# The sums of a float64 weight split move from GpSimd to TensorE and VectorE, and the state's decay to VectorE

## The chip, the cores and the metric

The kernel runs on one core of a Trainium2 chip. A core has TensorE (matrix products into PSUM, the accumulation memory), VectorE, ScalarE and GpSimd (arithmetic on SBUF, the on-chip memory of 128 partitions; VectorE and ScalarE read and write PSUM too), SyncE, which here only issues DMAs, and 16 DMA engines. The metric is the device time of one execution in microseconds, the median of three runs. In the profile TensorE's matmuls are called PE, its weight loads PEld, VectorE DVE, ScalarE ACT and GpSimd POOL.

## The reference

Three layers follow each other. All inputs are float32 but the dense layer's two weight matrices, which come as float64 values.

```python
# 1: attention with a decaying state, B=4, H=8, S=768, D=48
for t in range(S):
    kt, vt, rt, wt = k[:, :, t], v[:, :, t], r[:, :, t], w[:, :, t]
    cur = einsum('bhd,bhe->bhde', u[None] * kt, vt)
    y[:, :, t] = einsum('bhd,bhde->bhe', rt, state + cur)
    state = wt[:, :, :, None] * state + einsum('bhd,bhe->bhde', kt, vt)
x = y.transpose(0, 2, 1, 3).reshape(3072, 384)
# 2: dense layer, w_in 384x2048, w_out 2048x384
h = x @ w_in
x = (h * (1 / (1 + exp(-1.702 * h)))) @ w_out
# 3: eight experts (384 -> 1024 -> 384), 384 tokens each
logits = x @ w_gate       # all (token, expert) pairs, greatest first:
                          # a token goes to the first expert that has room
out[mask_e] = maximum(x[mask_e] @ w1[e], 0) @ w2[e]
```

## The kernel before

**Attention.** The 768 steps are cut into six chunks of 128; a chunk of one batch entry is a unit, 24 in all, each for all eight heads. Within a unit the products of the decays are formed by scans on VectorE (Q at L765, Fw at L769), k and r are scaled by them (L785, L788), and the state S of a batch entry (48 x 48 for each head) is carried from chunk to chunk: it is multiplied by the chunk's whole decay (L793, two instructions for the two halves of the heads) and the chunk's own part is added (L884). The three first units form the product r*k from what they have (L781), the others from a second copy of it in a tile nat_m (L812, L813, with u); its sums over a head (L815) are written on the diagonal of the score matrix by two `affine_select` masks on GpSimd (L822). A unit's result y goes into the dense layer as two fp32r tiles, hi (xh, L974, a rounding copy on ScalarE) and lo (xl, L977, the difference).

**Dense layer.** The 3072 tokens are eight blocks of 384, three units each. The hidden dimension is 16 slices of 128. A slot is one slice of one block: g1 (L1001, nine matmuls: three parts of the contraction by hi x hi, hi x lo, lo x hi), then the activation (L1047), its hi copy gh (L1050) and its difference gl on VectorE (L1053), and two slots later g2 (L1029, three parts of three matmuls, into acc). The slots come in this order: block 0 slices 0 to 7 (slots 0 to 7), block 1 (8 to 23), block 0 slices 8 to 15 (24 to 31), then blocks 2 to 7 (32 to 127). Slots 128 to 191 are the experts'.

**The float64 weights.** They come as 16 chunks of 128 x 768 (m = 0 to 15, w_in and w_out by turns, each good for two slices), and `split64` turns each into a hi and a lo tile in fp32r. The upper 32-bit words are rescaled (ScalarE L674, VectorE L678) and given their sign (L681); that is a, the value cut to its upper word. L687 and L688 form b, the part in the lower word. Then a + b (L692), hi = the rounding of it (ScalarE L696) and lo = (a + b) - hi (L699). At most two raw chunks are in flight; a is held in a ring of three tiles cvc, b in one of two cvb.

**The router's weights.** After the last chunk, `gate_weights` loads w_gate spread over the partitions, and `wog_steps` forms w_out times w_gate for each of the 16 slices: a sum hi + lo on GpSimd (L1137) and eight multiply-and-accumulate instructions on VectorE (L1141), 128 in all, then wogp (L1147, L1148). Block 7's matmuls begin only behind that.

**What sets the order.** The order of every engine's instructions is written at build time by a class `Issue`. It keeps a clock `t` and a time until which each engine is booked (`busy`: V, A, P for VectorE, ScalarE, GpSimd). The attention units, the chunks, the activations and the wog steps are chains of their own (Python generators), stepped by rank as the matmuls of the slots are laid down. `room(e, slack)` holds a chain until engine e is booked no further ahead than the slack. `either(lag, p, v)` gives an operation to GpSimd (cost p) or VectorE (cost v), whichever is done first by the booking, and by it L692, L699, L781, L785, L812 with L813 and L977 were placed. `until(cond)` holds the next slot's matmuls and puts a filler (`spin`, L638, a small bf16 matmul into an unused part of a bank) on TensorE for each 0.1 us of modelled waiting. On the chip only the order counts; the waits are by semaphores.

## Time and profile before

| | us |
|---|---|
| median of 3 runs | 937.81 |
| the runs | 935.88, 937.81, 937.83 |
| the profiled execution | 941.33 |
| its span, first to last instruction | 939.6 |
| TensorE busy (matmuls) | 882.1 (94%) |
| VectorE | 682.2 (73%) |
| ScalarE | 350.9 (37%) |
| GpSimd | 314.0 (33%) |
| mean granted TensorE clock | 0.947 |

The times are of one and the same kernel; the profiled execution has a time of its own, and sums over rows of its trace are to be set beside that. A share over the whole span says little here, since the stages have different limits; the stretches by slots are 41.6 to 97.8 us (slots 0 to 7), 97.8 to 128.0 (8 to 15), 128.0 to 195.1 (16 to 28), 195.1 to 519.8 (29 to 111), and what follows, which begins with the end of the router's weights.

### The profile page before, as it was taken

What the parts mean: (1) busy time and instruction counts of PE and PEld (TensorE: products, weight loads), DVE (VectorE), ACT (ScalarE), POOL (GpSimd) and SP (SyncE); (2) the same over time, 40 slices, a digit from 0 to 9 for tenths busy, and PEclk for the clock granted to TensorE, in tenths of its full rate; (3) what the DMA queues carried; (4) which work ended last, traced back from release to release, by engine and by line L of the source; (5) the groups of instructions that cost most, each with busy time, mean ns of one, the idle gap of its engine ahead of it and who ended that gap; (6) DMA issues with size and microseconds to landing.
All of it is one profiled execution on the core that took longest, in us unless ns stands there. A gap on an engine that the chain in (4) does not pass through costs nothing.

```text
span 939.6 us, 18095 instructions
## 1 busy us (share of the span) xinstructions
PE 882.1 (94%) x6867; PEld 834.0 (89%) x6867; DVE 682.2 (73%) x1791; ACT 350.9 (37%) x632; POOL 314.0 (33%) x319
## 2 busy tenths in 40 slices
PE   6977997999999999999999979989999989999995
PEld 5766996899999999999999979979889889899995
DVE  8699699799979789799797783666676776653210
ACT  1433553332333333333323034024554643657521
POOL 4477346512232324233223101021333423346311
PEclk8779999899999999999999999978898998899998
DMA  8526432423313222133210000058787977969900
GB/s 262 160 85 190 143 110 95 143 85 96 98 51 96 73 75 82 50 97 97 63 54 5 2 25 1 18 151 187 190 241 154 275 207 155 259 186 268 245 26 26
DMA packets 48504, 113.37 MB, mean 121 GB/s; under 512 B 7616, under 2 KB 13600, under 8 KB 48416
## 3 DMA queue, kind: packets, MB, share of 16 engines
q1 hardware_dynamic: 31680, 70.51, 23.8%
q0 software_dynamic: 12288, 34.61, 17.5%
q10 hardware_dynamic: 4448, 7.08, 2.2%
q8 instruction: 54, 0.88, 0.4%
q14 instruction: 34, 0.28, 0.1%
HBM read 75.95 MB, written 10.03 MB: 91 GB/s over the span
## 4 chain that ended last, share of the span: by engine, by line
PE 62%; DVE 20%; issue 9%; DMA 3%; POOL 2%; ACT 2%; ACTq 0%; DVEq 0%; POOLq 0%
PE g L1001 24%; PE acc L1029 22%; PE s L393 5%; DVE cvb L1078 3%; DVE cvb L1141 3%; PE s L920 2%; PE s L913 2%; DVE Q L765 2%; DVE gl L1053 2%; PE s L836 2%; DVE cvc L681 2%; PE acc L638 1%; DVE cvc L678 1%; PE s L453 1%; DMA hold<-in_w 1%
## 5 line engine op out<-in xcount | busy, mean ns | idle before, releaser
L1029 PE MATMUL acc<-wk,gh 128*128 128x384 f32 x1080 | 282.0, 341 | 0.3 <-ACT cva L1406 0.3
L1029 PEld LDWEIGHTS acc<-wk,gh 128*128 128x128 f32 x1080 | 196.5, 191 | 1.5 <-ACT cva L1406 0.6
L1029 PE MATMUL acc<-wk,gl 128*128 128x384 f32 x540 | 183.1, 339 | 0.0
L1001 PE MATMUL g<-xhb,wk 128*128 128x384 f32 x576 | 171.1, 350 | 11.0 <-DVE gl L1053 5.2
L1001 PE MATMUL g<-xha,wk 128*128 128x384 f32 x576 | 171.8, 350 | 6.9 <-DVE gl L1053 3.7
L1047 ACT ACTIVATE g<-g 128x384 f32<-128x384 f32 x128 | 60.8, 475 | 217.4 <-PE g L1001 195.4
L1001 PEld LDWEIGHTS g<-xhb,wk 128*128 128x128 f32 x576 | 108.8, 195 | 13.4 <-DVE gl L1053 5.6
L1001 PEld LDWEIGHTS g<-xha,wk 128*128 128x128 f32 x576 | 108.3, 193 | 10.7 <-DVE gl L1053 5.3
L1029 PEld LDWEIGHTS acc<-wk,gl 128*128 128x128 f32 x540 | 103.0, 191 | 0.0
L1001 PE MATMUL g<-xlb,wk 128*128 128x384 f32 x288 | 100.3, 348 | 0.0
L1001 PE MATMUL g<-xla,wk 128*128 128x384 f32 x288 | 99.4, 345 | 0.0
L1078 DVE SCALAR_TENSOR_TENSOR cvb<-cva,raw 128x384 f32<-128x384 f32 x168 | 95.6, 569 | 4.6 <-ACT cva L1117 1.5
L1053 DVE TENSOR_TENSOR gl<-g,gh 128x384 fp32r<-128x384 f32 x116 | 64.0, 551 | 39.3 <-ACT gh L1050 38.9
L1330 POOL DMA_DIRECT2D wk<-hold x64 | 57.6, 1045 | 85.3 <-ACT wk L1324 76.6
L1060 ACT ACTIVATE gh<-g 128x384 fp32r<-128x384 f32 x64 | 31.3, 489 | 129.0 <-PE g L1001 113.9
L1141 DVE SCALAR_TENSOR_TENSOR cvb<-cvb,raw 128x384 f32<-128x384 f32 x128 | 71.4, 557 | 10.8 <-POOL cvb L1137 5.1
L1063 DVE SCALAR_TENSOR_TENSOR gl<-g,gh 128x384 fp32r<-128x384 f32 x64 | 35.2, 552 | 60.7 <-ACT gh L1060 56.0
L793 POOL TENSOR_TENSOR S<-S,Q 48x192 f32<-48x192 f32 x40 | 49.4, 1235 | 88.6 <-DVE Q L765 87.1
L638 PE MATMUL acc<-ident 128*128 128x128 bf16 x842 | 60.1, 227 | 4.2 <-DVE ident L618 4.2
L638 PEld LDWEIGHTS <-ident 128*128 128x128 bf16 x842 | 51.4, 102 | 10.1 <-issue 5.1
L1050 ACT ACTIVATE gh<-g 128x384 fp32r<-128x384 f32 x116 | 56.9, 490 | 8.5 <-DVE cva L1112 3.2
L393 PEld LDWEIGHTS <-cvc 128*128 128x128 bf16 x840 | 53.3, 158 | 5.9 <-issue 2.6
(222 smaller groups left out, 1432.4 us busy)
## 6 DMA issues: line engine op xcount, KB each, us to landing
hold<-in_w SPq DMA_DIRECT2D x64, 384.0 KB
wk<-hold POOLq DMA_DIRECT2D x64, 384.0 KB
nat_m<-in_rk SPq DMA_DIRECT2D x20, 384.0 KB
raw<-in_w_in SPq DMA_DIRECT2D x8, 768.0 KB
raw<-in_w_out SPq DMA_DIRECT2D x8, 768.0 KB
nat_v<-in_v SPq DMA_DIRECT2D x22, 256.0 KB
nat_w<-in_w SPq DMA_DIRECT2D x22, 226.2 KB
nat_k<-in_k SPq DMA_DIRECT2D x22, 224.0 KB
```

What stands on the lines that cost most here:

```text
L393: nc.tensor.matmul(ps[:, :E], G[j], oh[:, j], start=(j == 0), stop=(j == NJ - 1))
L638: T.matmul(warm[0][:, Dm:], i16, i16, start=warm[1], stop=False, skip_group_check=True)
L793: P.tensor_tensor(h_, h_, Q[64 * s:64 * s + D, 1:HP * PW:PW, None].to_broadcast([D, HP, D]), op=OP.mult)
L1001: T.matmul(p, self.l1(kt, f, a), (self.xh, self.xl)[b_][:, kt], start=(kt == 0 and n == 0), stop=(kt == KT - 1 and n == 2))
L1029: T.matmul(self.acc[tt], gs[a][:, tt * C:(tt + 1) * C], self.r2(f, b_), start=(f in self.cuts and n == 0), stop=(end and n == 2))
L1047: A.activation(p, p, AF.Gelu_apprx_sigmoid)
L1050: A.activation(gh, p, AF.Copy)
L1053: V.tensor_tensor(gl, p, gh.bitcast(F32), op=OP.subtract)
L1063: V.scalar_tensor_tensor(gl, p, 0.0, gh.bitcast(F32), op0=OP.max, op1=OP.subtract)
L1078: V.scalar_tensor_tensor(scr[0][:, 0], x2, 1.0, wgB[e // 4][:, (e % 4) * Dm:(e % 4 + 1) * Dm], op0=OP.mult, op1=OP.mult, accum_out=router. ...
L1141: V.scalar_tensor_tensor(scr[0][:, 0], a, 1.0, wgB[e // 4][:, (e % 4) * Dm:(e % 4 + 1) * Dm], op0=OP.mult, op1=OP.mult, accum_out=wog[:, f ...
L1330: P.dma_start(out=Wlo[key].bitcast(F32), in_=raw, accum_op=OP.add)
```

## The change

For the first eight chunks (m < NPE = 8) hi is the rounding of a alone, without b. L688 writes b straight into the lo tile. Then, for each half of 384 columns, TensorE sums a (fp32, against the identity), -hi (against -I in fp32r) and b (against I in fp32r) in a PSUM bank of the ring s1 (three banks, shared with the attention units), and ScalarE copies the sum back over the lo tile. In the line numbers of the changed kernel the three matmuls are L704, L705 and L706 and the copy is L709. The tile cvb is free as soon as L688's form has been issued, and cvc after the second half.

For the chunks 8 to 15 the sum a + b and the difference stay two instructions, both on VectorE now (L719, L726). The decay of the state (L820 now), r*k (L808, or L839 with L840), the scaling of k (L812) and x's lo (L1004) are on VectorE too, without a choice. The masks (L849) stay on GpSimd. Two more constants hold I and -I in fp32r. The booked costs change with it, so the order of the filling work changes as well.

```diff
@@ -502,6 +502,7 @@
     DIRECT = 3
     NIN = 2
     DLAG = 1.5
+    NPE = 8
     NHOLD = 12
 
     consts = ctx.enter_context(tc.tile_pool(name="consts", bufs=1))
@@ -616,6 +617,9 @@
     dif = cv.tile([128, 128], F32, name="cva", bufs=NCVA)
     P.iota(dif, pattern=[[1, 128]], base=0, channel_multiplier=-1, allow_small_or_imprecise_dtypes=True)
     V.tensor_scalar(ident, dif, 0.0, None, op0=OP.is_equal)
+    identr = [s1p.tile([128, 128], F32R, name=f"identr{i}") for i in range(2)]
+    for t_, x in zip(identr, (1.0, -1.0)):
+        V.tensor_scalar(t_, dif, 0.0, x, op0=OP.is_equal, op1=OP.mult)
     later = s1p.tile([128, 128], U8, name="later")
     V.tensor_scalar(later, dif, 0.0, None, op0=OP.is_gt)
     lead = s1p.tile([R2, HP * PW + 1], U8, name="lead")
@@ -685,19 +689,42 @@
             ib = R["cvb"].new()
             b = cv.tile([128, KT * CW], F32, name="cvb", bufs=NCVB)
             V.tensor_scalar(b.bitcast(I32), ai, -8388608, None, op0=OP.bitwise_and)
-            V.scalar_tensor_tensor(b, low, 2.0 ** -52, b, op0=OP.mult, op1=OP.mult)
+            V.scalar_tensor_tensor(Wlo[key] if m < NPE else b, low, 2.0 ** -52, b, op0=OP.mult, op1=OP.mult)
+            if m < NPE:
+                R["cvb"].free(ib)
+
+                A.activation(Whi[key], a, AF.Copy)
+                sc.busy["A"] = max(sc.t, sc.busy["A"]) + 0.84
+                yield (("V", 1.5),)
+                load_w(m + 2)
+                for h in range(2):
+                    sl = slice(h * NB, (h + 1) * NB)
+                    ps, done = yield from bank()
+                    ps = ps[:, :NB]
+                    T.matmul(ps, ident, a[:, sl], start=True, stop=False)
+                    T.matmul(ps, identr[1], Whi[key][:, sl], start=False, stop=False)
+                    T.matmul(ps, identr[0], Wlo[key][:, sl], start=False, stop=True)
+                    yield (("T", 1.0),)
+                    yield from sc.room("A", 0.5)
+                    A.activation(Wlo[key][:, sl], ps, AF.Copy)
+                    done()
+                    sc.busy["A"] = max(sc.t, sc.busy["A"]) + 0.5
+                R["cvc"].free(ia)
+                yield 0.6
+                wdone.add(key)
+                return
             yield (("V", 1.4),)
             load_w(m + 2)
-            eng, step = yield from sc.either(VLAG)
-            eng.tensor_tensor(a, a, b, op=OP.add)
+            yield from sc.room("V", 0.3)
+            V.tensor_tensor(a, a, b, op=OP.add)
             R["cvb"].free(ib)
-            yield step
+            yield (("V", 0.95),)
             yield from sc.room("A", 0.3)
             A.activation(Whi[key], a, AF.Copy)
-            yield (("A", 0.73),)
-            eng, step = yield from sc.either(VLAG)
-            eng.tensor_tensor(Wlo[key], a, Whi[key].bitcast(F32), op=OP.subtract)
-            yield step
+            yield (("A", 0.83),)
+            yield from sc.room("V", 0.3)
+            V.tensor_tensor(Wlo[key], a, Whi[key].bitcast(F32), op=OP.subtract)
+            yield (("V", 0.95),)
             R["cvc"].free(ia)
             wdone.add(key)
 
@@ -777,22 +804,22 @@
             ia = R["At" + sf].new()
             At = [buf(f"At{s}", [128, HP, C]).rearrange("p (a t) -> p a t", a=HP) for s in range(2)]
             rk = At[0][:R2]
-            eng, step = yield from sc.either(DLG, 1.25, 0.6)
-            eng.tensor_tensor(rk, q, kk, op=OP.mult)
-            yield step
+            yield from sc.room("V", 0.3)
+            V.tensor_tensor(rk, q, kk, op=OP.mult)
+            yield (("V", 0.67),)
         yield from arrived(un, "k")
-        eng, step = yield from sc.either(KLAG, 1.25, 0.6)
-        eng.tensor_tensor(kk, kk, Q[:, 1:].rearrange("p (a t) -> p a t", a=HP)[:, :, 1:], op=OP.mult)
-        sc.after(step)
+        yield from sc.room("V", 0.3)
+        V.tensor_tensor(kk, kk, Q[:, 1:].rearrange("p (a t) -> p a t", a=HP)[:, :, 1:], op=OP.mult)
+        sc.after((("V", 0.67),))
         yield from arrived(un, "r")
         V.tensor_tensor(q, q, Fw.rearrange("p (a t) -> p a t", a=HP)[:, :, :C], op=OP.mult)
         R["Fw"].free(ifw)
         if c:
             for s in range(2):
                 h_ = St[64 * s:64 * s + D, s::2, :D]
-                P.tensor_tensor(h_, h_, Q[64 * s:64 * s + D, 1:HP * PW:PW, None].to_broadcast([D, HP, D]),
+                V.tensor_tensor(h_, h_, Q[64 * s:64 * s + D, 1:HP * PW:PW, None].to_broadcast([D, HP, D]),
                                 op=OP.mult)
-            sc.busy["P"] += 1.0
+            sc.busy["V"] = max(sc.t, sc.busy["V"]) + 0.7
         R["Q"].free(iq)
         dg = s1p.tile([128, H], F32, name="dg", bufs=2)
         if direct:
@@ -808,10 +835,10 @@
                 yield 0.1
             yield from arrived(un, "m")
             rk = nat_of("m", un)
-            eng, step = yield from sc.either(RLAG, 2.0, 1.0)
-            eng.tensor_tensor(rk[:, 0], rk[:, 0], rk[:, 1], op=OP.mult)
-            eng.tensor_tensor(rk[:, 0], rk[:, 0], uB.rearrange("p (h d) -> p h d", h=H), op=OP.mult)
-            yield step
+            yield from sc.room("V", 0.3)
+            V.tensor_tensor(rk[:, 0], rk[:, 0], rk[:, 1], op=OP.mult)
+            V.tensor_tensor(rk[:, 0], rk[:, 0], uB.rearrange("p (h d) -> p h d", h=H), op=OP.mult)
+            yield (("V", 1.1),)
             V.tensor_reduce(dg, rk[:, 0], axis=AX.X, op=OP.add)
             yield (("V", 0.5),)
             free(un, "m")
@@ -973,9 +1000,9 @@
             xh, xl = yield from place()
             A.activation(xh, y[:, :KT], AF.Copy)
             yield (("A", 0.5),)
-            eng, step = yield from sc.either(XLAG, 0.95, 0.47)
-            eng.tensor_tensor(xl, y[:, :KT], xh.bitcast(F32), op=OP.subtract)
-            yield step
+            yield from sc.room("V", 0.5)
+            V.tensor_tensor(xl, y[:, :KT], xh.bitcast(F32), op=OP.subtract)
+            yield (("V", 0.5),)
             R["y" + sf].free(iy)
             xdone[blk] = xdone.get(blk, 0) + 1
         if un == EARLY[-1]:
```

The order of the instructions shows it at three places. First GpSimd, from the masks of the first units on, before: `cvc` is a, `wk` a weight tile (or, in a mask or a product, a tile of an early unit), `S` a state.

```order
L822 AFFINE_SELECT At_370<-dg 128x512
L822 AFFINE_SELECT At_371<-dg 128x512
L699 TENSOR_TENSOR wk<-cvc,wk 128x768
L906 COPY wk<-wk 128x6x16
L692 TENSOR_TENSOR cvc<-cvc,cvb 128x768
L699 TENSOR_TENSOR wk<-cvc,wk 128x768
L692 TENSOR_TENSOR cvc<-cvc,cvb 128x768
L812 TENSOR_TENSOR wk<-wk 128x384
L813 TENSOR_TENSOR wk<-wk,uB 128x384
L699 TENSOR_TENSOR wk<-cvc,wk 128x768
L822 AFFINE_SELECT wk<-dg 128x512 x2
L692 TENSOR_TENSOR cvc<-cvc,cvb 128x768
```

The same stretch now, up to the sum of the first wog step (L1164):

```order
L849 AFFINE_SELECT At_376<-dg 128x512
L849 AFFINE_SELECT At_377<-dg 128x512
L933 COPY wk<-wk 128x6x16
L849 AFFINE_SELECT wk<-dg 128x512 x2
L849 AFFINE_SELECT At_858<-dg 128x512
L849 AFFINE_SELECT At_859<-dg 128x512
L849 AFFINE_SELECT wk<-dg 128x512 x2
L849 AFFINE_SELECT At_1763<-dg 128x512
L849 AFFINE_SELECT At_1764<-dg 128x512
L1164 TENSOR_TENSOR cvb<-wk 128x384
```

All sums, products and decays between the masks have left GpSimd.

On TensorE two half sums of one chunk now stand between the parts of a g2 (`acc`), ahead of the next slot's g1 (`g`):

```order
L1056 MATMUL acc_619<-wk,gl 128x384
L704 MATMUL s_628<-cvc,ident 128x384
L705 MATMUL s_628<-wk,identr_137 128x384
L706 MATMUL s_628<-wk,identr_136 128x384
L1056 MATMUL acc_620<-wk,gh 128x384 x2
L1056 MATMUL acc_620<-wk,gl 128x384
L1056 MATMUL acc_621<-wk,gh 128x384 x2
L1056 MATMUL acc_621<-wk,gl 128x384
L704 MATMUL s_653<-cvc,ident 128x384
L705 MATMUL s_653<-wk,identr_137 128x384
L706 MATMUL s_653<-wk,identr_136 128x384
L1028 MATMUL g_658<-xhb,wk 128x384
```

Sixteen such triples are in the program, four ahead of slot 0's g1 and twelve between it and slot 8's.

On VectorE the third place is the end of the router's weights, behind the last gl of block 6 (`gl<-g`, L1053; `raw` is w_gate, of which each of two tiles holds four experts). Before, 39 multiply-and-accumulate instructions, in one row of three and nine of four:

```order
L1053 TENSOR_TENSOR gl<-g_5415,gh 128x384
L1141 SCALAR_TENSOR_TENSOR cvb,wog<-cvb,raw_1785 128x384 x3
L1141 SCALAR_TENSOR_TENSOR cvb,wog<-cvb,raw_1787 128x384 x4
L1141 SCALAR_TENSOR_TENSOR cvb,wog<-cvb,raw_1785 128x384 x4
...
L1141 SCALAR_TENSOR_TENSOR cvb,wog<-cvb,raw_1787 128x384 x4
L1148 TENSOR_TENSOR wogp<-wog,wogp 128x16x8
L1053 TENSOR_TENSOR gl<-g_5814,gh 128x384
```

And now, in 14 rows of four, 56:

```order
L1080 TENSOR_TENSOR gl<-g_5471,gh 128x384
L1168 SCALAR_TENSOR_TENSOR cvb,wog<-cvb,raw_1829 128x384 x4
L1168 SCALAR_TENSOR_TENSOR cvb,wog<-cvb,raw_1831 128x384 x4
...
L1168 SCALAR_TENSOR_TENSOR cvb,wog<-cvb,raw_1831 128x384 x4
L1175 TENSOR_TENSOR wogp<-wog,wogp 128x16x8
L1080 TENSOR_TENSOR gl<-g_6047,gh 128x384
```

Seventeen more of them stand behind block 6 and ahead of block 7's first gl, and the fillers ahead of block 7's first g1 rise from 327 to 483; those ahead of slots 2 to 8 go from 134 to 97.

## Rows read from the trace of the kernel before

**Rows 1.** Five stretches: length; busy time (instructions) of PE, PEld, DVE, ACT, POOL; clock, DMA

```profile
core 0: us, PE busy (x) PEld busy (x) DVE busy (x) ACT busy (x) POOL busy (x), PEclk, DMA share, GB/s
41.60:97.80 56.20, 45.07 (x415) 40.62 (x414) 54.05 (x63) 21.75 (x38) 37.80 (x24) 0.88 0.38 117
97.80:128.00 30.20, 29.37 (x181) 28.86 (x180) 22.99 (x29) 16.56 (x30) 13.56 (x7) 1.00 0.43 134
128.00:195.10 67.10, 58.74 (x467) 55.46 (x468) 59.33 (x96) 24.50 (x44) 33.73 (x25) 0.92 0.39 127
195.10:519.80 324.70, 323.76 (x2335) 312.25 (x2333) 278.10 (x707) 106.03 (x222) 93.50 (x93) 1.00 0.24 70
519.80:549.80 30.00, 24.77 (x365) 24.45 (x364) 23.04 (x81) 1.86 (x5) 3.99 (x4) 1.00 0.01 2
```

**Rows 2.** The fillers of L638 in two stretches: length; PE, PEld busy

```profile
41.60:97.80 56.20, 7.43 (x116) 6.58 (x116) 0.88 0.38 117
519.80:549.80 30.00, 18.42 (x327) 18.25 (x327) 1.00 0.01 2
```

**Rows 3.** The tail: VectorE’s L1141 as one group, then single instructions by start and length

```profile
L1141 DVE SCALAR_TENSOR_TENSOR cvb<-cvb,raw 128x384 f32<-128x384 f32 x39 | 21.7, 557 | 5.9 <-POOL cvb L1137 4.7
...
520.52 0.56 DVE L1141 SCALAR_TENSOR_TENSOR cvb<-cvb,raw 128x384 f32<-128x384 f32 x1
521.12 0.56 DVE L1141 SCALAR_TENSOR_TENSOR cvb<-cvb,raw 128x384 f32<-128x384 f32 x1
525.26 0.56 DVE L1141 SCALAR_TENSOR_TENSOR cvb<-cvb,raw 128x384 f32<-128x384 f32 x1 [1.17 <-POOL cvb L1137]
...
549.76 0.69 PE L1001 MATMUL g<-xhb,wk 128*128 128x384 f32 x1 [5.23 <-DVE gl L1053]
```

**Rows 4.** Instructions of a line: count, shortest/median/longest in ns, first and last start

```profile
L681 DVE SCALAR_TENSOR_TENSOR cvc<-raw,cvc x16: 927/958/2609, 22.2 to 161.5; 128x768 int32<-128x768 int32 x16
L687 DVE TENSOR_SCALAR cvb<-cvc x16: 531/556/1922, 23.2 to 164.1; 128x768 int32<-128x768 int32 x16
L688 DVE SCALAR_TENSOR_TENSOR cvb<-raw,cvb x16: 957/959/2480, 23.8 to 164.7; 128x768 f32<-128x768 uint32 x16
L1053 DVE TENSOR_TENSOR gl<-g,gh x116: 525/552/559, 47.9 to 583.3; 128x384 fp32r<-128x384 f32 x116
```

**Rows 5.** The same view of the difference L699 on GpSimd and on VectorE

```profile
L699 POOL TENSOR_TENSOR wk<-cvc,wk x13: 1820/2151/2738, 34.1 to 168.2; 128x768 fp32r<-128x768 f32 x13
L699 DVE TENSOR_TENSOR wk<-cvc,wk x3: 959/1134/1683, 93.9 to 169.1; 128x768 fp32r<-128x768 f32 x3
```

**Rows 6.** VectorE by form, 41.6 to 97.8: count, busy us, mean ns, idle before

```profile
L681 DVE SCALAR_TENSOR_TENSOR cvc<-raw,cvc 128x768 int32<-128x768 int32 x6 | 8.2, 1360 | 0.0
L688 DVE SCALAR_TENSOR_TENSOR cvb<-raw,cvb 128x768 f32<-128x768 uint32 x6 | 6.7, 1113 | 0.2
L687 DVE TENSOR_SCALAR cvb<-cvc 128x768 int32<-128x768 int32 x6 | 5.4, 907 | 0.0
```

**Rows 7.** VectorE by form, 128.0 to 172.2

```profile
L681 DVE SCALAR_TENSOR_TENSOR cvc<-raw,cvc 128x768 int32<-128x768 int32 x4 | 6.2, 1553 | 0.1
```

**Rows 8.** Timeline from 32.4 to 34.9: start, length, instruction

```profile
32.44 1.68 POOL L822 TENSOR_SCALAR_AFFINE_SELECT At<-dg 128x512 f32<-128x512 f32 x2 [5.81 <-ACT dg L802]
32.74 0.88 DVE L687 TENSOR_SCALAR cvb<-cvc 128x768 int32<-128x768 int32 x1
33.66 1.27 DVE L688 SCALAR_TENSOR_TENSOR cvb<-raw,cvb 128x768 f32<-128x768 uint32 x1
```

**Rows 9.** The sum into the state, L884, as in Rows 4

```profile
L884 DVE TENSOR_TENSOR S<-s,S x32: 341/356/363, 77.0 to 427.6; 48x192 f32<-48x192 f32 x32
```

**Rows 10.** Timeline, TensorE: eight records of four fp32 matmuls

```profile
487.88 1.05 PE L913 MATMUL s<-nat_r,S 112*128 112x128 f32 x8
```

**Rows 11.** Timeline, VectorE: what ended the idle time in brackets

```profile
169.11 1.68 DVE L699 TENSOR_TENSOR wk<-cvc,wk 128x768 fp32r<-128x768 f32 x1 [1.92 <-ACT wk L696]
...
173.42 0.56 DVE L1141 SCALAR_TENSOR_TENSOR cvb<-cvb,raw 128x384 f32<-128x384 f32 x1 [2.63 <-DMA raw<-in_w_gate]
```

## The prediction

> **What bounds the kernel now.** I read the busy shares first, then the windows of five stretches, in each of them the engine that is nearly full, then VectorE's instructions there by form, and last the waits. In the windows [rows 1] the reader is to see three kinds of stretch. From 41.6 to 97.8 us (slots 0 to 7) VectorE works 54.05 of 56.20 us and TensorE 45.07, of which 7.43 are fillers [rows 2]: VectorE bounds. From 97.8 to 128.0 (slots 8 to 15) and from 195.1 to 519.8 TensorE works 29.37 of 30.20 and 323.76 of 324.70: TensorE bounds, and VectorE's work there is free as long as it keeps up (278.10 of 324.70). From 128.0 to 195.1 (slots 16 to 28) VectorE works 59.33 of 67.10 and TensorE 58.74: neither is full, and VectorE's 7.8 us of idle time are waits. From 519.8 to 549.8 TensorE spends 18.42 us on 327 fillers [rows 2] and then waits 5.23 us for a gl, while VectorE works off the router's weights [rows 3]: VectorE bounds again. What follows 549.8 keeps its order and its price.
>
> VectorE's work up to slot 28 takes longer than it needs. The same instruction on the same shape lasts very differently there: L681 from 927 to 2609 ns, L687 from 531 to 1922, L688 from 957 to 2480 [rows 4]. The long ones lie under GpSimd's sums, which take about 2 us each [rows 5]; gl, which reads PSUM, stays between 525 and 559 wherever it stands [rows 4]. If each form is given its shortest time, L681, L687 and L688 alone lose 2.6, 2.2 and 0.9 us in the first stretch, and the window's 25 forms together 14.3 us [rows 6]. The same subtraction gives 5.1 us between 97.8 and 128.0, where TensorE hides it, 10.9 between 128.0 and 195.1 (there four of L681 take 6.2 us in place of 3.7 [rows 7]), and 12.1 in the long stretch, where TensorE hides it as well.
>
> **What the change takes away.** GpSimd loses 92 instructions: 14 sums of L692, 13 of L699, 40 half decays of L793, 6 products, 19 differences of L977. Most of the stretching goes with them; what stays are the masks. Their price is read where a pair of them ran beside VectorE before the next sum began: L687 took 0.88 in place of 0.53 and L688 1.27 in place of 0.96 [rows 8], 0.66 us for the pair. Some four pairs stand before slot 8 and three more before slot 28, about 2 us in each stretch. The relief is therefore some 12 us before slot 8 and 9 in slots 16 to 28.
>
> **What it adds to VectorE.** Prices: a 128x768 sum 0.96 (L699 on VectorE at its shortest [rows 5]), half a decay 0.36 (L884, of the same shape [rows 9]), an x difference and each rk product 0.55 (the 128x384 of gl [rows 4]). Up to slot 7: four half decays 1.4, two more pairs of products 2.2, one sum fewer, the two small identities about 0.5: +3.1 us. Slots 8 to 15: one sum, two differences of weights and one of x, 3.4, hidden by TensorE. Slots 16 to 28: ten sums and differences where one was, +8.6; six half decays +2.2; a pair of products +1.1; two x differences +1.1; and three of L1078 and three wog products that now stand later, -3.6: together +9.3. Long stretch: 30 half decays 10.8 and 16 x differences 8.8, under a TensorE that leaves VectorE 46.6 us of room. It is this work that costs nothing there, and its cover is large enough even if each took twice as long.
>
> **What it adds to TensorE.** Sixteen half sums, each one plain fp32 matmul against the identity and two in fp32r, 384 columns each. Four fp32 matmuls of 128 columns took 1.05 us in eight records [rows 10]; if fp32 costs by columns, 384 are worth six records of 0.13, 0.79 us. The 181 matmuls of slots 8 to 15 took 29.37 us, 0.16 each [rows 1], so two fp32r ones cost 0.32. A half sum is then 1.1 us. The bounds: 0.48, if the fp32 matmul costs no more than the others, and 1.9, twice what I take for it; I take 1.0, since the eight records hold the start of a row of matmuls too. Twelve half sums stand between slots 0 and 7: 12 us. Fillers before slots 2 to 8 go from 134 to 97, which takes 37 x 0.064 = 2.4 us off. TensorE's work in the first stretch becomes 45.07 - 2.4 + 12 = 54.7 of 56.2 us: the change lowers VectorE's floor there (54.05 - 12 + 3.1 = 45) and puts TensorE's nearly where VectorE's was. ScalarE's half copies lie on an engine that works 21.75 of 56.2.
>
> **First stretch: -4 us,** between -1.5 (TensorE's 54.7) and -11 (VectorE's 45). TensorE's 45.07 were taken at a granted clock of 0.88, so its floor may be lower; but the half sums stand between the parts of g1 and g2 in a fixed order and wait for ScalarE's hi and VectorE's lo, so I stay on TensorE's side of the middle. The start and slots 8 to 15 I put at 0: in the latter TensorE is full.
>
> **Slots 16 to 28: -5.5 us.** VectorE's work comes out as it was, 59.3 - 9 + 9.3 = 59.6. What shrinks is its idle time. Two waits hang on GpSimd's queue of sums: 1.92 us for a hi that comes late because its sum was GpSimd's, and 2.63 us for the load of the gate's weights, which is issued when the last chunk is done [rows 11]; 4.55 of the 7.8. I add 1 us for TensorE's waits on the same chunks. The bounds are 0 and -7.5 (67.1 - 59.6).
>
> **Long stretch: -1 us.** TensorE works 323.76 of 324.70; no more than these 0.9 us can go.
>
> **The tail: +13 us.** The order says how many of the 128 wog products stand behind the last gl of block 6: 39 before, 56 now, since VectorE's other work stands ahead of them (three fewer come before slot 28, fourteen fewer after). They run 0.60 us from start to start, and at each GpSimd sum between groups of eight VectorE waits 1.17 [rows 3]. Seventeen more cost 10.2, and 2.4 more sums 2.8: +13.0. The gl of slot 112 is queued behind all of them on VectorE, and g2 and g1 wait for it. TensorE does not cover it: its fillers there rise from 327 to 483, at 18.42/327 = 0.056 each 27.2 us, with 6.4 of real matmuls 33.6, against some 41 of VectorE. The bounds are +10.2 (sums hidden) and +14.2 (one more wait).
>
> **Sum.** -4 - 5.5 - 1 + 13 = +2.5 us against the profiled execution's 941.33. The median of the runs is 937.81, 3.5 us below that one; carried over, 940.3.
>
> A page has a rule that speaks against the masks. The Trainium skill, "SBUF — State Buffer", section "Who interferes with whom", says that VectorE and GpSimd share one pair of ports as an exclusive lock: a VectorE instruction with two SBUF inputs collides with a GpSimd one that reads SBUF, and the loser is blocked entirely. The trace agrees for gl, which has one SBUF input and does not stretch; the pair of masks that ran 1.68 us and cost VectorE 0.66 agrees only in part. By the rule in full the front would gain 7 us less, by the row it stays.
>
> **Rivals.** A is the forecast, +2.5, its own range -0.5 to +5.5 (937.3 to 943.3).
> B: the whole relief comes back. The half sums fall into TensorE's gaps (11 us in the first stretch), and both stretches come near VectorE's floors, -10 and -7; with -1 and +13 that is -5, 932.8 (931 to 935). For it: VectorE is plainly the fullest engine, 54.05 of 56.20. Against it: by my sum TensorE is left 1.5 us.
> C, the other side: TensorE becomes the bound of the first stretch. It decides from 1.13 us for a half sum, where TensorE's sum passes 56.2; at 1.9 it is 65.5, +9.3, and halfway +4.6: 4.6 - 5.5 - 1 + 13 = +11.1, 948.9. For it: fp32 columns are dear [rows 10], and a half sum stops what stands behind it in the order. Against it: the way over GpSimd that it replaces takes 4 us for each chunk.
> D: the masks alone keep VectorE out for as long as they run: seven pairs at 1.68 us in place of 0.66 are 7.1 back, +9.6, 947.4. Against it: the pair in [rows 8], under which both instructions went on.
>
> Chances: A 0.50, B 0.28, C 0.13, D 0.09. A difference below 0.2% (1.9 us) can't be told from none here. Of A 0.28 lies above it, 0.20 within and 0.02 below; B is faster in 0.25 and within in 0.03; C is slower; D is slower in 0.05 and, where B's relief comes with it, within in 0.04. Together: faster 0.27, same 0.27, slower 0.46. The range 932 to 949 holds A, D, most of B and half of C.
>
> **What would show it.** Right: L681 and L687 of before's numbering near 0.95 and 0.55 under everything but masks, and VectorE below 50 us busy in slots 0 to 7; a half sum's three matmuls near 1 us; slots 16 to 28 in some 61 us; one run of 56 wog products of about 41 us and TensorE waiting over 6 us for the gl behind it. If the first stretch falls by 9 us or more, B holds; if it is longer than 56 us with TensorE full, C. The forecast is wrong at its largest term if the tail is not longer by 10 to 14 us.

## The result and the profile after

| | before | after | forecast |
|---|---|---|---|
| median of the runs, us | 937.27 | 951.26 | 940.3 (932 to 949) |
| lowest, highest | 935.88, 937.83 | 945.75, 954.74 | |
| profiled execution | 941.33 | 950.17 | |
| its span | 939.6 | 948.4 | |

The ratio of the times is 1.0134, with an interval of 1.0104 to 1.0164: slower. The forecast said slower too, by 2.5 us; the profiled executions lie 8.8 us apart and the medians 14.0, and the time is outside the range.

The two traces are laid beside each other by the start of a slot's g1 (L1001 before, L1028 after): 41.6, 101.9, 128.1, 195.1, 516.7 and 549.8 us before, and 43.6, 100.6, 125.7, 192.4, 511.8 and 557.5 after, for slots 0, 8, 16, 28, 111 and 114.

| stretch | before, us | after, us | change | forecast |
|---|---|---|---|---|
| to slot 0 | 41.6 | 43.6 | +2.0 | 0 |
| slots 0 to 7 | 60.3 | 57.0 | -3.3 | -4 |
| 8 to 15 | 26.2 | 25.1 | -1.1 | 0 |
| 16 to 27 | 67.1 | 66.7 | -0.4 | -5.5 |
| 28 to 110 | 321.5 | 319.5 | -2.1 | -1 |
| 111 to 113 (the tail) | 33.1 | 45.7 | +12.6 | +13 |
| the rest | 389.9 | 390.9 | +1.0 | 0 |
| sum | | | +8.7 | +2.5 |

The stretches of [rows 1] carry wrong slot numbers: in that trace slot 7's g1 begins at 97.8, slot 8's at 101.9 and slot 28's at 195.1, so that those windows hold slots 0 to 6, 7 to 15, 16 to 27 and 28 to 111. The forecast of -4 was made on slots 0 to 6; they went from 56.2 to 53.1 us. Here are the five middle stretches of the table, first before (length, busy time and count of PE, PEld, DVE, ACT, POOL, granted clock, DMA):

```profile
41.60:101.90 60.30, 49.17 (x451) 44.56 (x450) 55.42 (x66) 24.06 (x43) 40.50 (x26) 0.89 0.39 122
101.90:128.10 26.20, 25.29 (x149) 24.95 (x146) 21.72 (x26) 14.25 (x26) 10.87 (x6) 1.00 0.40 125
128.10:195.10 67.00, 58.72 (x467) 55.43 (x468) 59.23 (x95) 24.50 (x44) 33.73 (x25) 0.92 0.39 127
195.10:516.70 321.60, 320.66 (x2317) 309.31 (x2316) 277.00 (x704) 105.07 (x220) 93.25 (x93) 1.00 0.24 71
516.70:549.80 33.10, 27.87 (x383) 27.39 (x381) 24.14 (x84) 2.83 (x7) 4.24 (x5) 1.00 0.01 2
```

and in the changed kernel:

```profile
43.60:100.60 57.00, 54.47 (x463) 46.66 (x461) 43.62 (x70) 28.00 (x54) 5.86 (x6) 0.97 0.39 129
100.60:125.65 25.05, 25.05 (x147) 25.05 (x145) 20.56 (x30) 13.74 (x27) 0.00 (x0) 1.00 0.39 119
125.65:192.35 66.70, 60.88 (x513) 57.06 (x513) 55.87 (x104) 23.46 (x44) 5.61 (x7) 0.95 0.40 127
192.35:511.80 319.45, 318.86 (x2315) 309.60 (x2315) 273.36 (x720) 106.86 (x221) 30.34 (x44) 1.00 0.24 72
511.80:557.50 45.70, 36.64 (x540) 36.16 (x538) 34.86 (x122) 2.82 (x7) 6.99 (x7) 0.94 0.01 2
```

In the first row the bound has changed hands: VectorE, 55.42 of 60.30 before, is busy 43.62 of 57.00, and TensorE, 49.17 before, 54.47. In the third TensorE and VectorE are busy 60.88 and 55.87 of 66.70, and the granted clock is 0.95.

The long instructions of [rows 4] and the pair of masks of [rows 8], in the changed kernel (a line: count, shortest/median/longest ns; then the timeline):

```profile
L685 DVE SCALAR_TENSOR_TENSOR cvc<-raw,cvc x16: 934/955/1268, 22.3 to 151.0; 128x768 int32<-128x768 int32 x16
L691 DVE TENSOR_SCALAR cvb<-cvc x16: 533/553/560, 23.3 to 152.7; 128x768 int32<-128x768 int32 x16
L820 DVE TENSOR_TENSOR S<-S,Q x40: 341/353/357, 66.6 to 492.2; 48x192 f32<-48x192 f32 x40
```
```profile
73.03 1.54 POOL L849 TENSOR_SCALAR_AFFINE_SELECT At<-dg 128x512 f32<-128x512 f32 x2 [9.13 <-PE s L706]
73.28 0.80 DVE L682 TENSOR_SCALAR cvc<-cvc 128x768 int32<-128x768 int32 x1
74.11 1.27 DVE L685 SCALAR_TENSOR_TENSOR cvc<-raw,cvc 128x768 int32<-128x768 int32 x1
```

The stretching is gone: the longest L685 lasts 1268 ns where L681 reached 2609. The pair of masks costs VectorE 0.27 + 0.34 = 0.6 us of its 1.54. Half a decay takes 0.353 us.

One half sum in the timeline of TensorE, between two parts of a g2:

```profile
52.18 0.34 PE L1056 MATMUL acc<-wk,gl 128*128 128x384 f32 x1
52.35 0.81 PE L704 MATMUL s<-cvc,ident 128*128 128x384 f32 x2
52.70 0.63 PE L705 MATMUL s<-wk,identr 128*128 128x384 f32 x1
53.17 0.34 PE L706 MATMUL s<-wk,identr 128*128 128x384 f32 x1
53.35 0.51 PE L1056 MATMUL acc<-wk,gh 128*128 128x384 f32 x2
```

From start to start it is 53.35 - 52.35 = 1.00 us. Since records of neighbours overlap, the starts tell the price: L706 to the next is 0.18, so the fp32 matmul (two records) takes about 0.65.

The tail, to be set against [rows 3]: VectorE's products as one group, and the matmul that waits for the gl behind them.

```profile
L1168 DVE SCALAR_TENSOR_TENSOR cvb<-cvb,raw 128x384 f32<-128x384 f32 x56 | 31.2, 557 | 8.8 <-POOL cvb L1164 7.1
557.47 0.69 PE L1028 MATMUL g<-xhb,wk 128*128 128x384 f32 x1 [9.06 <-DVE gl L1080]
```

There are 56, six waits for GpSimd sums make 7.1 us, and TensorE, having worked off 483 fillers in 27.14 us, stands 9.06 us in place of 5.23.

### The profile page after: what moved, and what is told of

It reads as the page before. It is cut to its first block, busy times and chain, and to the rows that moved or that the text cites. A ratio compares the mean times of both kernels' runs of the same rounds, so it can differ in the third digit from the quotient of the medians.

```text
span 948.4 us, 18514 instructions
## 1 busy us (share of the span) xinstructions
PE 900.9 (95%) x7096; PEld 850.6 (90%) x7096; DVE 675.2 (71%) x1869; ACT 357.9 (38%) x648; POOL 173.3 (18%) x227
## 4 chain that ended last, share of the span: by engine, by line
PE 70%; DVE 13%; issue 7%; DMA 6%; POOL 2%; ACT 2%; ACTq 0%; POOLq 0%; DVEq 0%
PE g L1028 26%; PE acc L1056 25%; PE s L393 5%; DVE cvb L1168 4%; PE s L863 3%; PE s L947 2%; PE s L940 2%; DVE cvb L1105 2%; DMA cvb<-x2d,idx 1%; PE s L453 1%; PE s L704 1%; DMA wk<-hold 1%; DVE gl L1080 1%; PE acc L642 1%; DMA hold<-in_w 1%
## 5 line engine op out<-in xcount | busy, mean ns | idle before, releaser
L1056 PEld LDWEIGHTS acc<-wk,gh 128*128 128x128 f32 x1080 | 199.1, 193 | 2.4 <-issue 1.3
L1028 PE MATMUL g<-xhb,wk 128*128 128x384 f32 x576 | 170.4, 346 | 13.6 <-DVE gl L1080 11.5
L1028 PE MATMUL g<-xha,wk 128*128 128x384 f32 x576 | 172.3, 350 | 7.3 <-ACT wk L723 2.4
L1028 PEld LDWEIGHTS g<-xhb,wk 128*128 128x128 f32 x576 | 107.3, 191 | 15.0 <-DVE gl L1080 12.0
L1028 PEld LDWEIGHTS g<-xha,wk 128*128 128x128 f32 x576 | 108.2, 193 | 10.1 <-ACT wk L723 2.6
L1028 PE MATMUL g<-xla,wk 128*128 128x384 f32 x288 | 99.5, 345 | 0.0
L1028 PE MATMUL g<-xlb,wk 128*128 128x384 f32 x288 | 99.1, 344 | 0.1
L1105 DVE SCALAR_TENSOR_TENSOR cvb<-cva,raw 128x384 f32<-128x384 f32 x168 | 93.0, 554 | 3.9 <-ACT cva L1144 0.6
L849 POOL TENSOR_SCALAR_AFFINE_SELECT At<-dg 128x512 f32<-128x512 f32 x42 | 31.7, 777 | 329.1 <-DVE dg L842 286.2
L1090 DVE SCALAR_TENSOR_TENSOR gl<-g,gh 128x384 fp32r<-128x384 f32 x64 | 35.2, 552 | 60.8 <-ACT gh L1087 60.7
L642 PE MATMUL acc<-ident 128*128 128x128 bf16 x1007 | 70.3, 226 | 4.2 <-DVE ident L619 4.2
L642 PEld LDWEIGHTS <-ident 128*128 128x128 bf16 x1007 | 61.0, 102 | 10.7 <-issue 5.6
```

What stands on the lines that cost most here:

```text
L642: T.matmul(warm[0][:, Dm:], i16, i16, start=warm[1], stop=False, skip_group_check=True)
L849: P.affine_select(At[s], dg[:, s::2][:, :, None].to_broadcast([128, HP, C]), pattern=[[0, HP], [1, C]], compare_op=OP.is_equal, fill=0.0, ...
L1028: T.matmul(p, self.l1(kt, f, a), (self.xh, self.xl)[b_][:, kt], start=(kt == 0 and n == 0), stop=(kt == KT - 1 and n == 2))
L1056: T.matmul(self.acc[tt], gs[a][:, tt * C:(tt + 1) * C], self.r2(f, b_), start=(f in self.cuts and n == 0), stop=(end and n == 2))
L1090: V.scalar_tensor_tensor(gl, p, 0.0, gh.bitcast(F32), op0=OP.max, op1=OP.subtract)
L1105: V.scalar_tensor_tensor(scr[0][:, 0], x2, 1.0, wgB[e // 4][:, (e % 4) * Dm:(e % 4 + 1) * Dm], op0=OP.mult, op1=OP.mult, accum_out=router. ...
```

## The experiments

Each median is set against runs of the kernel before on the same chip in the same session; there were three sessions, with medians of 939.53, 937.14 and 939.19 us for the kernel before, and a difference across them is less sure than one within. Ratios are with their 95% intervals. "Products" are the 128 wog products.

### Where the 12.6 us of the tail and the missing 5 us of slots 16 to 27 come from

**Decay and x differences undone.** The two blocks go back to their form before:

```diff
-                V.tensor_tensor(h_, h_, Q[...].to_broadcast([D, HP, D]), op=OP.mult)
-            sc.busy["V"] = max(sc.t, sc.busy["V"]) + 0.7
+                P.tensor_tensor(h_, h_, Q[...].to_broadcast([D, HP, D]), op=OP.mult)
+            sc.busy["P"] += 1.0
...
-            yield from sc.room("V", 0.5)
-            V.tensor_tensor(xl, y[:, :KT], xh.bitcast(F32), op=OP.subtract)
-            yield (("V", 0.5),)
+            eng, step = yield from sc.either(XLAG, 0.95, 0.47)
+            eng.tensor_tensor(xl, y[:, :KT], xh.bitcast(F32), op=OP.subtract)
+            yield step
```

> The changed kernel with two of its parts undone: the state's decay on GpSimd again and the x differences placed by the old rule. 39 products stand behind block 6 in place of 56. Theory T: the tail shrinks by 12.6 us and the front stays, 951 becomes 938 to 940. Rival (the front's lost gain is VectorE's moved work): the front gains another 4 us or more, 934 or less. Rival (the loss lies in TensorE's clock or elsewhere): over 945.

Measured: 932.53 against 939.53, ratio 0.9913 (0.9887 to 0.9939). In its trace the tail is 33.1 us, as before to the tenth, and slots 16 to 27 take 60.8 in place of 66.7. So T and its first rival hold a part each: 12.6 us are the tail's, and another 5.9 us of the front were lost to these two parts.

**The decay alone undone** (the first four lines of that diff).

> The changed kernel with the state's decay alone on GpSimd again; the x differences stay on VectorE. 48 products stand behind block 6 (56 in the changed kernel, 39 with both parts back). Theory T: the tail shrinks by 8 x 0.60 and one GpSimd sum, about 6 us. If the decays are what held up slots 16 to 28 (they are 6 of the 8 instructions that the two parts add there), these slots take some 61 us in place of 66.6 and the whole is 939; if the x differences are, they take 66 and the whole is 945.

Measured: 932.47 against 937.14, ratio 0.9940 (0.9922 to 0.9959). The tail is 39.7 us with its 48 products, 6.0 less than with 56; slots 16 to 27 take 61.0. It is the decay that holds up slots 16 to 27, by 5.7 us. The whole came out below 939: of the 15.6 us between its trace and the changed kernel's 11.6 are these two, and 3.4 lie behind slot 114 (387.5 us in place of 390.9), where the order is the same.

**The decay on VectorE, but not booked.**

```diff
-            sc.busy["V"] = max(sc.t, sc.busy["V"]) + 0.7
```

> The changed kernel with one line out: the state's decay stays on VectorE, but VectorE is not booked for it when the order is made. The order of TensorE's matmuls and fillers is then that of the experiment with the decay back on GpSimd (932.5), with the decays' 0.7 us a unit on VectorE. Theory O (the order that the booking makes cost 5 us in slots 16 to 28, not the decays' time on VectorE): these slots take 61 to 62 us and the whole is 932 to 935. Rival (VectorE's time): 66 us and 938 or more.

Measured: 934.81 against 939.19, ratio 0.9948 (0.9929 to 0.9966). The order of TensorE's instructions is that of the experiment ahead, slots 16 to 27 take 62.1 us, and the tail takes 39.7 as there, with the decays on VectorE. So by these traces 4.6 of the 5.7 us are the order and 1.1 the decays' time, and the tail's 6.0 are the order's too. What the order does is read from the two timelines of TensorE. First the changed kernel:

```profile
146.76 4.53 PE L642 MATMUL acc<-ident 128*128 128x128 bf16 x78
153.72 0.44 PE L1028 MATMUL g<-xha,wk 128*128 128x384 f32 x1 [2.43 <-ACT wk L723]
155.17 0.62 PE L1028 MATMUL g<-xha,wk 128*128 128x384 f32 x2 [0.84 <-DVE wk L726]
159.65 1.17 PE L863 MATMUL s<-nat_r,nat_k 48*128 48x128 f32 x16
169.59 0.45 PE L1028 MATMUL g<-xhb,wk 128*128 128x384 f32 x1 [2.41 <-DVE gl L1080]
```

and the one with the decay undone:

```profile
147.21 1.29 PE L642 MATMUL acc<-ident 128*128 128x128 bf16 x20
148.43 1.16 PE L863 MATMUL s<-nat_r,nat_k 48*128 48x128 f32 x16
153.04 0.43 PE L947 MATMUL s<-At,nat_v 128*64 128x128 f32 x2 [1.06 <-DVE At L870]
155.02 1.79 PE L642 MATMUL acc<-ident 128*128 128x128 bf16 x29
```

In both, slot 22 is held for the last chunks (it begins at 153.72 and 156.62). In the second an attention unit's matmuls (L863 and what follows) fill that time. With the decay booked on VectorE the unit is put behind the beginning of slot 22, 78 fillers stand in its place, its matmuls (about 4 us) come on top afterwards, and slot 24 waits 2.41 us for a gl. The fillers of the whole stretch are 116 and 123, the other matmuls the same. The windows of that stretch with the decay undone, and then with the decay unbooked, are to be set against the third row of the changed kernel's above:

```profile
125.90:186.90 61.00, 58.37 (x521) 55.13 (x520) 55.88 (x99) 23.32 (x44) 13.37 (x13) 1.00 0.43 140
```
```profile
123.30:185.40 62.10, 58.24 (x520) 55.06 (x519) 56.85 (x105) 23.30 (x44) 5.88 (x7) 1.00 0.43 137
```

VectorE works 55.87 us in the changed kernel and 55.88 with the decay undone: its load is not the cause. TensorE stands idle 66.70 - 60.88 = 5.8 us against 2.6, and is busy 2.5 us longer for the same work, at a granted clock of 0.95 against 1.00.

The second part is not the same in every execution. The order of the changed kernel stands, slots 16 to 27 unaltered, in three more traces: the changed kernel again, and the doubled and the cheap half sum below. All have the same three waits of TensorE (5.6 us); these are the longest and, of the two shortest, the cheap one:

```profile
123.51:192.49 68.98, 63.32 (x513) 59.67 (x513) 55.83 (x104) 23.54 (x44) 5.22 (x7) 0.90 0.38 123
118.56:183.38 64.82, 59.10 (x513) 56.00 (x513) 55.89 (x104) 23.56 (x44) 5.43 (x7) 0.97 0.41 131
```

So this order takes 64.8 to 69.0 us, by the granted clock, and the orders made without the decay's booking 60.8 to 62.1 in five traces, all at 1.00. The gap holds, at 2.7 to 8.2 us; 2 to 3 of them are the added idle time, the rest TensorE's slower work.

### What the half sums cost

**The detour alone** (the changed `split64` for m < 8; the sums of the other chunks, the products, the decays and the x differences as before, each in the form of the kernel before).

```diff
+            if m < NPE:
+                ...
+                return
```

> The kernel before with the way over TensorE for the first eight chunks alone: the decays are on GpSimd, the other sums, products and x differences are placed by the old rule. 39 products stand behind block 6, as before. Theory D (the half sums eat on TensorE what VectorE gains): the front gains 2 to 4 us, 933 to 936. Rival R (the half sums are cheap and the decays and sums moved to VectorE eat the gain): the front gains 8 us or more, 929 or less. Rival C (the detour itself lies on the path): slower than before, 940 or more.

Measured: 938.83 against 939.53, ratio 0.9987 (0.9966 to 1.0009): the same. Its trace is its fastest run (933.80); there slots 0 to 7 take 55.9 us, 4.4 less than before, and slots 16 to 27 take 66.9, no less. The trace speaks for D, the times tell no difference from before.

**No detour** (decay and x differences undone, and):

```diff
-    NPE = 8
+    NPE = 0
```

> As the experiment with decay and x differences back on GpSimd, but with no chunk over TensorE: all 16 chunks have both sums on VectorE. 39 products behind block 6 in both. VectorE gets 16 sums of 0.95 more before slot 8, 15 us, and TensorE loses 16 half sums. Theory D (the half sums take on TensorE what they spare VectorE): within 3 us of 932.5. Rival (the detour is a real gain over sums on VectorE): slower by 6 us or more, 938 and up.

Measured: 935.31 against 937.14, ratio 0.9979 (0.9956 to 1.0002): 1.8 us below the kernel before, where the first experiment lay 7.0 below its own. Slots 0 to 7 take 63.9 us and the start 40.8, where with the detour (first experiment) they take 58.3 and 43.0. VectorE is busy 56.46 of 63.9 there. By the traces slot 8 begins 3.4 us later (104.7 against 101.3); by the medians, each against its own session's, the detour is worth 5: between the two theories, though the time itself lies within D's 3 us. The detour takes 14.7 us off VectorE there (56.5 against 41.8 in the first experiment), and gives back about a third of them.

**The fp32 matmul twice.**

```diff
+                    T.matmul(ps, ident, a[:, sl], start=True, stop=True)
                     T.matmul(ps, ident, a[:, sl], start=True, stop=False)
```

> The changed kernel with the fp32 matmul of each half sum issued twice (the second starts the sum anew). Theory D (TensorE bounds the front): 12 x 0.65 = 7.8 us more before slot 8, of which 5 to 8 are seen, 956 to 959. Rival (half sums lie in TensorE's idle time): 951 to 953.

Measured: 958.48 against 939.53, ratio 1.0184 (1.0140 to 1.0227).

**The fp32 matmul made cheap.**

```diff
-                    T.matmul(ps, ident, a[:, sl], start=True, stop=False)
+                    T.matmul(ps, identr[0], Whi[key][:, sl], start=True, stop=False)
```

> The changed kernel with the fp32 matmul of each half sum replaced by a fp32r one on the hi tile (this leaves out the part of a that its rounding drops), 0.17 us in place of 0.65. Theory D: 12 x 0.48 = 5.8 us less TensorE before slot 8, of which 3 to 6 are seen, 943 to 947. Rival (doubling the matmul cost, but VectorE stands close behind TensorE): 948 to 951.

Measured: 936.49 against 939.19, ratio 0.9984 (0.9961 to 1.0006). Slots 0 to 7 in the windows of the two (doubled, then cheap):

```profile
44.70:109.30 64.60, 62.14 (x487) 51.30 (x485) 43.86 (x70) 28.02 (x54) 5.86 (x6) 0.97 0.35 116
```
```profile
41.70:93.50 51.80, 47.27 (x451) 43.32 (x449) 43.45 (x70) 28.21 (x54) 5.87 (x6) 1.00 0.44 147
```

Against the 57.0 us of the changed kernel they are +7.6 for 12 x 0.65 = 7.8 us added, and -5.2 for 12 x 0.48 = 5.8 taken away; VectorE works 43.5 to 43.9 in all three. The changed kernel's second trace has 55.4 there, which makes them +9.2 and -3.6. What a half sum costs on TensorE is paid there, in whole or for the most part: TensorE is the bound of slots 0 to 7 in the changed kernel. The four half sums ahead of slot 0 pay too: it starts at 41.7 with cheap ones and at 44.7 with doubled ones. The whole fell by more than the 3 to 6 expected: of the 14.6 us between its trace and the changed kernel's 9.0 lie ahead of slot 28, and 5.6 behind slot 114, where the order is the same.

### Whether the tail can be had back

**All products ahead.**

```diff
-                yield from sc.room("V", 0.4)
+                yield from sc.room("V", 0.7)
```

> The changed kernel, with one number of the order altered: a wog product is let onto VectorE when VectorE is booked up to 0.7 us ahead in place of 0.4. By that all 128 products stand ahead of the last gl of block 6 (56 stood behind it), and 98 fillers move ahead of slots 34 and 48. Theory T (the tail sets the loss): the 41 us run of products between slots 111 and 114 goes, slots 111 to 114 take some 10 us in place of 45.7, VectorE has 47 us of idle time in the long stretch to take them, so 951 falls to 915 to 922, below the kernel before. Rival (VectorE is late in the long stretch as well): the products in front delay the gl and attention work, TensorE waits there, and no more than 15 us come back, 936 or more.

Measured: 929.11 against 939.53, ratio 0.9873 (0.9814 to 0.9932); its four runs lie in two pairs, near 924.5 and 934, and the trace is of the latter. Slots 111 to 113 take 9.4 us in place of 45.7, as T has it; but the long stretch takes 337.6 in place of 319.5, 18 us more, of which TensorE's 98 fillers are a part and 9 us are waits, 5.1 of them for one cva (L1139). Both theories hold a half.

**Half of them ahead,** with decay and x differences undone: the same line with 0.5.

> As the experiment with decay and x differences back, and a wog product is let onto VectorE when it is booked up to 0.5 us ahead in place of 0.4: 16 products behind block 6 in place of 39, no fillers ahead of slots 29 to 111. Theory T: 23 products and three sums fewer, 13.8 + 3.5, minus nothing in front: 932.5 becomes 915 to 918. Rival (products further ahead hold up gl and the attention units in the long stretch, as in the first experiment): 925 or more.

Measured: 916.18 against 937.14, ratio 0.9770 (0.9739 to 0.9800), the fastest of all, as T has it. (The rival's "first experiment" is the one with all products ahead.) Its windows over the long stretch and the tail:

```profile
186.00:512.80 326.80, 321.76 (x2316) 309.00 (x2316) 297.85 (x754) 105.26 (x220) 89.17 (x95) 1.00 0.24 70
512.80:529.80 17.00, 17.00 (x192) 16.84 (x191) 11.92 (x41) 3.12 (x7) 2.00 (x2) 1.00 0.01 2
```

In the tail TensorE is full: its fillers outlast the 16 products, and it waits for no gl. The long stretch gives back 5 us (326.8 against 321.9 with the products late, from 187.2 to 509.1).

**The kernel before with 0.5.**

> The kernel before with the one number altered (a product is let onto VectorE at 0.5 us of booking in place of 0.4): 12 products behind block 6 in place of 39, nothing else moved. Theory T: 27 products and three sums fewer, 16.2 + 3.5 us, 918 to 921, so that nearly the whole gain of the best version is the tail's and not the change's. Rival: the products in front hold up the long stretch, 928 or more.

Measured: 934.24 against 939.19, ratio 0.9948 (0.9925 to 0.9971): T failed. The tail fell from 33.1 to 15.3 us, 17.8 of the 19.7 that were expected, but the long stretch grew by 13.1 (334.6 against 321.5). TensorE waits 9.5 us there, where it waited 0.9 before: 4.4 for a masked At, 4.2 for a gl (four times) and 0.9 for a cva; the longest for an At and for a gl:

```profile
369.77 0.45 PE L1001 MATMUL g<-xha,wk 128*128 128x384 f32 x1 [1.63 <-DVE gl L1053]
380.29 1.16 PE L913 MATMUL s<-nat_r,S 112*128 112x128 f32 x8 [2.13 <-DVE At L843]
```

So the number alone is worth 5 us, the parts of the change without decay and x differences 7 (the first experiment), and the two together 21. Which of those parts lets the long stretch bear the products was not tried apart.

**The wait where it is used,** on top of "half of them ahead".

```diff
-                if blk == NBLK - 1:
-                    sc.until(lambda: todo[1])
...
+            if f2 == 0:
+                sc.until(lambda: todo[1])
             thin_logits(f2, ps)
```

> As the experiment with 16 products behind block 6, but the order waits for the router's weights only where they are used, before the matmul of slot 114, and not before block 7: no product stands behind block 6's last gl, some stand between the gl of slots 112 and 113. Theory T: another 5 to 10 us, 907 to 912. Rival (TensorE's fillers, 157 ahead of slot 115, and the products between the gls cost as much): 915 to 918.

Measured: 933.62 against 939.19, ratio 0.9938 (0.9917 to 0.9960): worse than either theory. The waiting moved to the matmul that uses the weights:

```profile
543.79 0.66 PE L1234 MATMUL s<-gh,wogp 128*128 128x384 f32 x1 [13.24 <-DVE wogp L1175]
```

The last piece of the weights (L1175) comes at 543.4 us, where with half of them ahead it comes at 527.1: VectorE now has 24 instructions of block 6's logits (L1105, 14.1 us) among the last 16 products.

### The changed kernel again

> The changed kernel once more, beside the kernel before on the same chip. Its first runs lay 14 us above before's by the medians, the two profiled executions only 8.8. If before's profiled execution was merely a slow one of its kind (941.3 against 937.3), the medians differ by 11 to 14 again; if the changed kernel's first runs were slow ones, by 8 to 10.

Measured: 948.52 against 937.14, ratio 1.0104 (1.0066 to 1.0143), 11.4 us by the medians. Its trace has the same stretches within 2.3 us, and the tail is 45.7 again. The kernel before ran between 932.74 and 941.13 in that session, and its profiled execution of 941.33 was slower than any of them, so the first expectation holds. (In the two other sessions single runs of it took up to 942.23.)

## Why the prediction failed, step by step

**VectorE's relief** was right: the long instructions shrank to their shortest, the masks that stayed cost 0.6 us a pair (0.66 was taken), and VectorE's work in slots 0 to 7 fell by 11.8 us, to 43.6 (9 was worked out: 12 of relief less 3.1). Rival D's price is out: a pair of 1.54 us cost 0.6, and the four chunk instructions that met a mask lost 1.2 us in all. Its mechanism is not out, and I read [rows 8] too weakly. When L682 began, the first mask had some 0.4 us to run, and it lost 0.27; L685 lost 0.34 under the rest of the second. GpSimd's sums show the same in the kernel before:

```profile
64.97 2.09 POOL L699 TENSOR_TENSOR wk<-cvc,wk 128x768 fp32r<-128x768 f32 x1 [1.23 <-ACT wk L696]
65.27 2.61 DVE L681 SCALAR_TENSOR_TENSOR cvc<-raw,cvc 128x768 int32<-128x768 int32 x1
```

L699 had 1.79 us to run when L681 began, and L681 took 2.61 - 0.93 = 1.68 us more than its shortest. In that trace 25 of VectorE's chunk instructions began under a GpSimd instruction with more than 0.15 us left, and each lasted longer by what was left less 0.11 to 0.15 us. That fits the Trainium skill's rule in "SBUF — State Buffer", "Who interferes with whom", that the loser is blocked entirely: it waits for the rest of the other, nearly to its end. Gl, with one SBUF input, does not stretch, as the rule has it.

**TensorE's price** was right: 1.0 us for a half sum, 1.00 measured. Slots 0 to 6 were given -4 and came to -3.1 (slots 0 to 7 to -3.3, and to -4.9 in the second trace); the doubled and the cheap half sum show that it was TensorE's floor that set them, as the forecast had it. Rivals B (the whole relief) and C (a half sum over 1.13 us) are out: C's sign, a stretch over 56 us, is to be read on slots 0 to 6, at 53.1.

**The start at 0** was wrong by 2.0 us (1.4 in the second trace). Four half sums stand ahead of slot 0, and I counted only the twelve behind it; with cheap ones slot 0 starts at 41.7 as before.

**Slots 16 to 28 at -5.5** (slots 16 to 27) is the step that failed: -0.4, and +1.9 in the second trace. I took VectorE's work there (59.6 forecast, 55.9 found) and its two waits behind GpSimd's sum and the gate's load; both waits went as I said, and without the decays' booking the same stretch took 62.1, which is -5.0. What I left out is that a booked cost does not only take VectorE's time but moves other work: a unit's matmuls left the time ahead of slot 22, where they cost nothing, 78 fillers took their place, and the unit came later on a full TensorE. With the booking TensorE stood idle 5.8 us there, without it 2.6, and its granted clock was 0.90 to 0.97 in place of 1.00; its waits on the chunks, for which I had taken 1 us off, were 3.3. The order shows it (fillers ahead of slot 22: 71 before, 78 after, 63 with the decay undone, where 25 stand ahead of slot 25); I had read only the places up to slot 8 and the tail.

**The long stretch at -1** came to -2.1, past my bound of 0.9, since TensorE's busy time itself fell by 1.8 us; why stays open. **The tail at +13** came to +12.6: 17 products more at 0.60 and two more waits for a GpSimd sum at 1.18. Undoing decay and x differences takes it back to 33.1 us.

**The carrying over** from the profiled execution to the median was the other mistake. I took 3.5 us off because the kernel before's profiled execution was that much slower than its median. The changed kernel's profiled execution, 950.17, lies 1.1 below its median. Of the 14.0 us between the first medians 8.8 are in the two traces; the rest is that before's traced run was longer than its others, and the scatter of the runs. That scatter goes with the granted clock (the changed kernel: 944.97 us at 0.961, 954.74 at 0.948). A part of it lies in slots 16 to 27 (64.8 to 69.0 us in the same order), a part behind slot 114, which took from 385.3 us (cheap half sum) to 391.5 (doubled) in the traces, in the same order; the +1.0 us there is within it.

## What to carry to other kernels

Where an order is made at build time from booked costs, moving an operation to another engine is two changes: its time, and the order of everything that is booked around it. Read the order at each place where the bounding engine waits, not only where the moved instructions stand; here 18 us (12.6 in the tail, 5.7 in slots 16 to 27) were lost by way of the order and, in the second, of the clock that followed, while the prices of the moved instructions had been right (half a decay 0.353 for 0.36, a half sum 1.00 for 1.0). And compare medians with medians: a single profiled execution says where the time goes, not how far two kernels lie apart, and one stretch can differ between two executions of the same kernel (slots 16 to 27: 66.7 and 69.0).

## What the hardware showed beyond that

- A plain fp32 matmul against a stationary 128 x 128 over 384 columns takes two records and 0.65 us, against 0.17 to 0.18 for a fp32r one of the same shape: nearly four times as long.
- Half a decay (48 x 192, two SBUF inputs) takes 353 ns on VectorE; on GpSimd, in the kernel before, the same instruction took 1235 ns on average (40 instructions, 49.4 us; 506 to 1847).
- After TensorE had stood 2.41 us in slot 24 of the changed kernel, its granted clock was 0.57 over the next 4 us, which is nearly its lower level (1.2 of 2.4 GHz), and six matmuls of g1 took 2.0 us in place of 1.0; from 174.0 it was 1.00 again. In the trace of the cheap half sum the same wait at the same place (2.40 us) left the clock at 1.00. The same instructions, up to the next part of g1 behind the unit's matmuls, took 4.27 us behind the first wait and 2.73 behind the second, so that the one cost some 1.5 us more than its length and the other did not.
